# Engine assignments of 714 operations read from a table, beside a new order of operations

## The chip, the cores and the metric

One core of a Trainium2 chip runs the whole program. The metric is the device time of one execution in microseconds (us), as the median of several runs. The core has TensorE (PE, matrix products, with its weight loads shown apart as PEld), VectorE (DVE), ScalarE (ACT), GpSimd (POOL) and SyncE (SP, which issues most transfers). Each engine runs its own instructions strictly in the order in which the program gives them.

## The reference

Three stages follow each other; all is float32 at the boundary.

```
q, k, v: 4 batches x 8 heads x 576 rows x 64          (attention)
  q, k rotated by position (cos, sin tables); scores = q k^T / 8
  attn = exp(scores - rowmax) / (rowsum + 1e-9);  x = attn v      -> 2304 x 512
h = x w_in;  g = max(h,0) + alpha*min(h,0);  y = g w_out           w_in 512x2048, w_out 2048x512
soft mixture of experts over y: logits = y phi (32 slots),
  softmax over tokens -> slot inputs;  8 experts: relu(s w1) w2;  softmax over slots -> output 2304 x 512
```

## The kernel before, in words

The program first lists some five thousand operations (`op(engine, cost, due, function, ...)`), each a small group of instructions on one engine, with what it depends on and which buffers it takes. `Plan.order` then decodes a compressed text, `ORDER`, into a permutation of that list, checks that it respects dependencies and buffers, and the operations are emitted in that order. So the order in each engine's queue, and in SP's queue of transfers, is written out in full; the engine of an operation is fixed in the code. The `cost` and `due` arguments no longer decide anything.

**Weights of the first layer** (`prep_w`): eight pieces of w_in arrive as 64-bit floats and are turned to float32 by three DVE steps (lines 673, 675, 677); ACT finds the bound (685), scales to a float16 high part (688), makes a scaled diagonal `dg` (`split`, 244), PE subtracts (250, 251), and ACT copies the low part (256). Eight more pieces, of w_out, get the same three DVE steps. **Queries and keys** (`prep_qk`): for each of 4 batches and 4 head pairs, POOL multiplies by the two tables (334) and adds (337, or 342 in batch 0). In batches 1 to 3 the sum is split in a high part (ACT: 350 for keys, 352 for queries) and a low part (POOL: 357, 359), and ACT spreads the key's high part into four places (362). **Rows** (`row_events`): PE makes scores (434 in batch 0; 443 to 447 later), DVE finds the negated maximum (452), ACT takes exp with its sum (457), ACT adds 1e-9 (473), DVE takes the reciprocal (474), POOL multiplies (498, and 497 for the tail rows). In batch 0 PE transposes the result (521, 572) and ACT copies it out (531, 576); in batches 1 to 3 DVE transposes blocks (508, 542) and two transfers through memory finish the turn. **Attention times v** (`pv_events`): PE (604), then ACT writes the high part (614), DVE the low part (617). **First layer** (`chunk_events`): 9 blocks of 256 tokens by 16 chunks; PE makes 12 products (766), ACT takes the relu of the negated sum into `rl` (774), DVE forms `g` (779), DVE transposes pairs of chunks (795). After a block, PE makes logits (803) and slot sums (958). The experts come at the end, with their weights loaded once the attention buffers are closed.

The functions that the change touches, and what calls them:

Of the kernel before, what the change touches and what calls it, by code (L numbers as in the profile page):

```python
# [33 lines left out]

ORDER = (
    "c-"
    "mD~2Urx>7M?S+yX?|2bX1gHRZyNvF=9a}V#E>@e8EKHdzz>u8ly;*XDo>rC5a`L_$(MD8XHRS0TQez(t;?`EHove%L2mg&b(V@7u@+~=FUCm{O3RC+`Z@i<x|abJZJsVy~d{s04%K9(G"
    "#p5cvrJp?-$T9|GpAT1M<P-C2u>bTnSxvZPu*P%=hF%DB+-"
    "VM46wm=jF&ILo=DhV{ip!cO{G+{s63(N><uEvE&r1mrieoYPWW|iK^2+XZnj$Uz27Jrnxf^ioBWu?3NsAdF}qf$WisAbkTn!I>5qOecZ|1?~w^uR{2T0tH8TxQu(NI%Y=Dj{k6^Q-"
    "VZE!jve0A;#KVfVEwWLrZ)|~3L0Mkd&rtsVy`qCeSAp$D7X$r9(6wO${w0S>Wd}*kQ1Wp02Amo_P=JPa&f8q6In+h?!L+v!BZZ;sRMi$ulBqgUt?X>2mw7Qsj4ayWk3r&54e}N+vuqh{"  # L40
    "u=y`y9|u%gPb9$Co<>t7~b?Nvu+Ej98oFrtGEY4{F?@AjSS)b=*jsdV-60n0yd-"
    "`I^UR&=xlE?Q}VSRLq*5L!)_CbhP(ab99pC`4=e}CIh!C2SiWv(UJQqp98$Tq1~xzlJR4eT(BM@)e9R5-"
    "?S@9Vyy8ww^Quy)ALf|}#=v@l^5Iheug<KEgRVdH>ikF9B!I@}Aq!6|j8BihxbdNKE<Axd^RmM;T)@?&)S~3ap{t#jpR0WH7-s)5yBvZl!56NFJj-`}?p5~hF<XP5$DNRX-"
    "O<TzP0(d*e^>>JjhX|$N&uzX_St{Tw1;12n8Wd<qdr~k&)2%%2rI7vhrMf3A=*tjp-3{eSljuNVFp{j_LGyxVNQ2=@$ax>WaXNO?RnSF?B0}VvLZ^pvg-"
    "hBRHCIdv%MTfR;*jTH|$!<CU>y)H<SNn;jf&XsMz$-rS6eO`Ztx&OUm{uA=7`_?G*MB#GI&lS{wRiTGvZhe(CI-Xo2UmBe_f=I!8SNzJBfTRkPLAiCGZtx%~APyVmXdJTufR)-"
# [12 lines left out]
    "Q4g}hu13IjPIG&u8fkXOw(5dKuTHG{<^pi{0?pswGGc*B)4lCK0Iq3{;PHLp@E4a<OEO`{SIYUS-{!#j9UAGW1(3Jzc5{1K;q)gq)70#(<doq5DOxAkUQfP;GThV##S6^ZuM9FW+n-"
    "Ta`RuccBhT2y*G03i<;i|IBov;8dba$7yeUl&$Cw|RY5rzXahr^ffKzj0lAEsv4@-}4>*0pAfL-gv%NGZ8!W^iL$$?4LvB%!V9S&Z4??BuxH{}8&h-;l^(sF%4pL-oVHG?-"
    "!4fd^I)jG6wyzIPJwXuoHB!BYHA6f1ET*fM#7A?=44Qvm1KVg7Td9rtnj2)q|+h|x#p9wfV^XUHSpJ48GCIaA!Y1kue*(_GZJ{rod+TUB-"  # L60
    "r<!nQ9F#x}<V|p?8(kk&?ZL^)%KTvD+r<mR1-8(9e8Wp$C~2Ko9C0h?cZXd^6>P2vj0eaz7y}jX!e;!ec{4JHq16OYZ{P+5wHd>=t4!|)!Na3a3_rsin04NE=-tWHp-"
    "`lep$tm6KBR4+;SE@U?KR}NZs%5TuD3A;RhzBx?-5TPIGa^SytxMwiDa<$r5(#TJmWws0pJQ8oo>Bvz^ZtemghKD1qK`o|1<0{4dW!*!r<41U_GAu`%Zv;n-"
    "yrKZMIJhSg7)}d13prV>ByBxxUuH+TF3&lvburu1!Or??8x&mDv-G3%6xx9B6VRy&nMVW@Bv-%NBcyR`T7tANmZ|yyfJ)=0doU=5m8;>w0dz;YZT+__e>bTP3DJ+mWQLNhpr1S-"
    "T`(f9ecJKCV5owHDcDFKckwwR&f(Y|)P^O>B~ePD!|)QKL9ta6H1Y%VODPXg~d>{L8I!mXm%UwcHJgURaPJSMxKk^3j+2<Pe$7@kJBZHo3XdqFFAN_ZqI>2AbT+D^YXK!=jn9djEj=Q}"
    "TM@dw>VNg%h>FRrx^KxDu7Zk8i9A=Pgysj(@n%7oP^txn((w1Z$wbSFgZ8VxBuzBej9&*QefpJz1@(?>ux4iHbbj_ODf%Dd9#i?B0NtZ(5yBz8QoDd;gvf*&hO%wxX(f9zaFHQMmiDKf"
    "tHPQ#1EI@^}Pq+Fe+eMdn>xl$#qsCb-t3>xVDjvrxXQ35E`>LOtZU(V&jr9w%t^eg#k+SnSi_P;KTQ?=$V@-"
    "m(S;odzK5G6pCa1NvXysB(zxkx6=3FzAs=d*x~wBan*`$P@i^PdbNQJbD1p5`foD;u$g|3gUp#8DSg15)gno5D0{z)6~N=7?XVQx>-"
    "h)U=$GWjqLz^0xwcP=)Ax%I(F2dNP!3JmMUq1vgZYsvJf5Ud=O&j#yoYw0I$PFPc4B)BP`|_nhDH{7qDJ`Vg#O=5SomDWejFX-"
    "SJ|61)in@E8#H$!VYnm0*J2hr;Z2F5Oguf`WVp$yW&X}fPfNMUAgcib%donh-IM~IG?)oFruwUN=zOdXhjktAd%42ijfEmWv&Mn%Zl{`NiQ%GwM5Mb2uGquG6|y=@J&O<Dr$P^>L!*(1"
# [27 lines left out]
class Plan:  # L97
# [1499 lines left out]
```

## Time and profile before

| what | value |
|---|---|
| median of 3 runs | 570.95 us (568.36 to 573.3) |
| the profiled execution | 566.88 us, its span 565.1 us |
| busy over the span | PE 531.3 (94%), DVE 449.7 (80%), ACT 348.8 (62%), POOL 321.9 (57%) |
| chain that ended last | PE 75%, ACT 3%, DVE 2%, DMA 1%, issue 1% |
| granted TensorE clock | 0.996 of full speed over the span |
| transfers | 160.76 MB, mean 284 GB/s |

The span runs from the first to the last instruction. Busy time of PE is modelled at its ends. A row that names a line is a group of like instructions; the time after the bar is the group's sum and the mean of one.

### The profile page before, as it was taken

What the parts mean: (1) busy time and instruction counts of PE and PEld (TensorE: products, weight loads), DVE (VectorE), ACT (ScalarE), POOL (GpSimd) and SP (SyncE); (2) the same over time, 40 slices, a digit from 0 to 9 for tenths busy, and PEclk for the clock granted to TensorE, in tenths of its full rate; (3) what the DMA queues carried; (4) which work ended last, traced back from release to release, by engine and by line L of the source; (5) the groups of instructions that cost most, each with busy time, mean ns of one, the idle gap of its engine ahead of it and who ended that gap; (6) DMA issues with size and microseconds to landing.
All of it is one profiled execution on the core that took longest, in us unless ns stands there. A gap on an engine that the chain in (4) does not pass through costs nothing.

```text
span 565.1 us, 14815 instructions
## 1 busy us (share of the span) xinstructions
PE 531.3 (94%) x5770; PEld 394.9 (70%) x5770; DVE 449.7 (80%) x985; ACT 348.8 (62%) x879; POOL 321.9 (57%) x299
## 2 busy tenths in 40 slices
PE   3789998999999999999999999999999999999994
PEld 1455555678888787788787788868778888864463
DVE  5699978878998878889889798888864799843551
ACT  2799977899868767787786787667432222430131
POOL 0989996988989876887886787844300000001000
PEclk9999999999999999999999999999999999999998
DMA  8893945435899988698989789889665999899997
GB/s 300 309 361 118 328 123 181 135 119 167 293 337 333 332 282 314 194 333 287 327 294 339 252 287 319 266 262 327 226 227 179 411 407 406 290 372 391 403 327 226
DMA packets 80806, 160.76 MB, mean 284 GB/s; under 512 B 5344, under 2 KB 44640, under 8 KB 80736
## 3 DMA queue, kind: packets, MB, share of 16 engines
q1 hardware_dynamic: 79408, 158.99, 80.6%
q8 instruction: 46, 0.75, 0.5%
q10 hardware_dynamic: 1328, 0.82, 0.5%
q14 instruction: 24, 0.20, 0.1%
HBM read 115.75 MB, written 36.96 MB: 270 GB/s over the span
## 4 chain that ended last, share of the span: by engine, by line
PE 75%; ACT 3%; DVE 2%; DMA 1%; issue 1%; DVEq 0%; ACTq 0%
PE ph L766 33%; PE pv L604 11%; PE st L447 9%; PE pu L958 4%; PE lg L803 3%; PE ph L1289 2%; PE po L1348 2%; DMA ett<-sc 1%; PE st L443 1%; PE pf L1473 1%; PE st L445 1%; PE pt L521 1%; PE lgt L863 1%; ACT ks L362 1%; ACT e L457 1%
## 5 line engine op out<-in xcount | busy, mean ns | idle before, releaser
L766 PE MATMUL ph<-xt,w 128*128 128x256 f16 x1536 | 184.2, 273 | 0.5 <-DVE xt L617 0.5
L766 PEld LDWEIGHTS <-w 128*128 128x128 f16 x1728 | 161.9, 98 | 30.2 <-issue 7.4
L498 POOL TENSOR_SCALAR e<-e,mm 128x576 f32<-128x576 f32 x144 | 125.5, 881 | 70.3 <-DVE mm L474 66.7
L457 ACT ACTIVATE e<-st,mm 128x576 f32<-128x576 f32 x144 | 106.3, 739 | 37.1 <-DVE mm L452 31.3
L452 DVE TENSOR_REDUCE mm<-st 128x1 f32<-128x576 f32 x144 | 106.2, 742 | 20.1 <-PE st L447 11.7
L774 ACT ACTIVATE rl<-ph 128x256 f32<-128x256 f32 x144 | 53.5, 380 | 69.7 <-PE ph L766 63.9
L334 POOL TENSOR_TENSOR xn<-xn,tabs 128x576 f32<-128x576 f32 x60 | 89.4, 1502 | 6.9 <-DMA xn<-in_k_dram 3.0
L779 DVE SCALAR_TENSOR_TENSOR g<-rl,oma,ph 128x256 f32<-128x256 f32 x144 | 65.7, 465 | 21.3 <-ACT rl L774 20.6
L604 PE MATMUL pv<-ET,vt 128*64 128x256 f32 (+1 forms) x640 | 76.5, 384 | 0.1
L508 DVE STREAM_TRANSPOSE tb<-e 128x512 f32<-128x512 f32 (+1 forms) x108 | 74.8, 704 | 1.7 <-DMA sc<-tb 0.8
L447 PE MATMUL st<-ks,qs 128*128 128x288 f32 x384 | 74.6, 317 | 1.1 <-ACT ks L362 0.9
L604 PEld LDWEIGHTS pv<-ET,vt 128*64 128x64 f32 (+1 forms) x640 | 43.1, 136 | 25.8 <-issue 5.8
L447 PEld LDWEIGHTS st<-ks,qs 128*128 128x128 f32 x384 | 54.5, 189 | 4.6 <-issue 1.6
L795 DVE STREAM_TRANSPOSE gb<-g 128x512 f32<-128x512 f32 x64 | 43.9, 693 | 0.2
L434 PE MATMUL st<-ks 64*128 64x288 f32 (+1 forms) x168 | 30.2, 455 | 11.0 <-DVE ks L307 7.6
L978 POOL MEMSET edt<- 128x256 f32 x1 | 0.3, 313 | 68.4 <-DVE lp L947 68.4
L359 POOL TENSOR_TENSOR qs<-xn,qs 64x576 fp32r<-64x576 f32 x24 | 33.9, 1413 | 7.7 <-ACT qs L352 3.1
L337 POOL TENSOR_TENSOR xn<-xn 128x576 f32<-128x576 f32 x24 | 36.9, 1537 | 0.9
L362 ACT ACTIVATE ks<-xn 64x576 fp32r<-64x576 f32 x48 | 32.6, 680 | 0.7
L434 PEld LDWEIGHTS st<-ks 64*128 64x128 f32 (+1 forms) x168 | 17.2, 191 | 20.8 <-DVE ks L307 8.4
L614 ACT ACTIVATE xt<-pv,vb 128x256 f16<-128x256 f32 x32 | 15.1, 472 | 22.3 <-PE pv L604 21.5
L457 ACT ACTIVATION_READ_ACCUMULATOR e<-st,mm 128x1 f32 x144 | 28.5, 198 | 0.0
(171 smaller groups left out, 782.1 us busy)
## 6 DMA issues: line engine op xcount, KB each, us to landing
sc<-tb SPq DMA_DIRECT2D x48, 576.0 KB, 4.6
ET<-sc SPq DMA_DIRECT2D x24, 1152.0 KB, 7.3
xw<-in_moe_w_dram SPq DMA_DIRECT2D x42, 512.0 KB, 8.4
xn<-in_k_dram SPq DMA_DIRECT2D x15, 576.0 KB, 6.5
xn<-in_q_dram SPq DMA_DIRECT2D x15, 576.0 KB, 4.5
wraw<-in_moe_w_in_dram SPq DMA_DIRECT2D x8, 1024.0 KB, 8.4
wraw<-in_w_out_t_dram SPq DMA_DIRECT2D x8, 1024.0 KB, 6.0
wor<-in_moe_w_out_dram SPq DMA_DIRECT2D x16, 512.0 KB, 10.0
```

Source lines behind the costliest of these rows:

```text
L334: eng.tensor_tensor(e["x"][:, w], e["x"][:, w], tabs[:, w], ALU.mult)
L434: nc.tensor.matmul(st[to, j, at:at + w], x, k[rows, z:z + w], start=True, stop=True)
L447: nc.tensor.matmul(st[:, j, 0:288], r["q"][:, 768 * h + 128 * s:768 * h + 128 * s + 128].bitcast(F32R), r["k"][:, a, h, ks].bitcast(F32R), ...
L452: nc.vector.tensor_reduce(c["mm"][:, h:h + 1], c["st", h][:, :, 0:288], axis=AX.XY, op=ALU.max, negate=True)
L457: nc.scalar.activation(c["e"][:, h].rearrange("p (a n) -> p a n", a=2), c["st", h][:, :, 0:288], AF.Exp, bias=c["mm"][:, h:h + 1], accum_o ...
L498: nc.gpsimd.tensor_scalar(c["e"][:, h], c["e"][:, h], c["mm"][:, 6 + h:7 + h], 1.0, ALU.mult, ALU.mult)
L508: nc.vector.transpose(out=to if tail else to[:, :, 0:8].rearrange("p q (m h) j -> p q m h j", h=2)[:, :, :, h], in_=e.rearrange("p (m q j) ...
L604: nc.tensor.matmul(pv[r], v[k, 4 * h + i if i < 4 else 8 + (h if b else 0)], x, start=(i == 0), stop=(i == 4))
L766: nc.tensor.matmul(ph, wi[j][:, wp, kc, 128 * fo:128 * fo + 128], xt[:, xp, kc, :], start=(n == 0), stop=(n == 3 * KC - 1),)
L774: nc.scalar.activation(c["r"], c["ph"], AF.Relu, scale=-1.0)
L779: nc.vector.scalar_tensor_tensor(blk["g", j][:, fo, :], c["r"], oma[:, f:f + 1], c["ph"], ALU.mult, ALU.add)
L795: nc.vector.transpose(out=blk["gt", j // 2][:, f % 8 - 1:f % 8 + 1, :].rearrange("p c n -> p (c n)"), in_=blk["g", j][:, fo - 1:fo + 1, :] ...
```

## The change

A table of 714 digits, `ENGINES`, is added, and `plan.choose(a, b, ...)` reads the next digit and returns the engine at that place; digit 0 is in every place the engine that the operation had before. `ORDER` is replaced by another text. The helpers `copied` and `times` give the same copy or scaling on any of the engines. The transfers, the matrix products, the maxima, the exps and the transposes on DVE stay on their engines.

Counting the digits in the order in which the program reads them gives these assignments (before, then after):

| operation (line) | before | after |
|---|---|---|
| normalize a head's rows (498), 128 | POOL | POOL 65, ACT 57, DVE 6 |
| the same for tail rows (497 and 498), 16 | POOL | POOL 6, ACT 9, DVE 1 |
| add 1e-9 (473), 80 | ACT | ACT 58, DVE 22 |
| copy out transposes, batch 0 (531, 576), 56 | ACT | ACT 48, DVE 8 |
| high part of attention output (614), 48 | ACT | ACT 22, DVE 26 |
| multiply by tables (334), 60; add (337, 342), 30 | POOL | POOL 54, DVE 6; POOL 26, DVE 4 |
| high part of keys (350) 12, of queries (352) 24 | ACT | ACT 6, POOL 5, DVE 1; ACT 10, POOL 12, DVE 2 |
| low part of keys (357) 12, of queries (359) 24 | POOL | POOL 11, DVE 1; POOL 23, DVE 1 |
| spread keys (362), 48 | ACT | ACT 20, POOL 26, DVE 2 |
| relu of the negated sum (774), 144 | ACT | ACT 112, DVE 32 |
| weights: scale (688) 8, diagonal (244) 8, low part (256) 16 | ACT | ACT 7, DVE 1; ACT 3, POOL 5; ACT 14, DVE 2 |

In batch 0, 17 of 32 normalizations and 3 of 4 of the tail go to ACT, and 6 of the 18 table operations to DVE. Of the 32 relu that go to DVE, 15 are in blocks 0 to 5.

```diff
+ENGINES = (
+    "020000110000000002000200020012001000010202101121200120000012001011000000200020200100120002020011001000010102000002000000"
...
 ORDER = (
...
+    def choose(self, *engines):
+        self.chosen += 1
+        return engines[int(ENGINES[self.chosen - 1])]
...
+    def copied(on, dst, src):
+        if on == ACT:
+            nc.scalar.activation(dst, src, AF.Copy)
+        else:
+            engines[on].tensor_copy(dst, src)
+
+    def times(on, dst, src, scale):
+        if on == ACT:
+            nc.scalar.activation(dst, src, AF.Copy, scale=scale)
+        elif on == DVE:
+            nc.vector.tensor_scalar(dst, src, scale, None, ALU.mult)
+        else:
+            nc.gpsimd.tensor_scalar(dst, src, scale, 1.0, ALU.mult, ALU.mult)
...
-            o = op(on, cost, d, lambda mul=mul: mul(0), [o, *tabs_op], uses=[sx])
+            on = choose(POOL, DVE)
+            o = op(on, cost, d, lambda mul=mul, on=on: mul(0, on), [o, *tabs_op], uses=[sx])
...
-                        o = op(ACT, 640, d + LEADS[0], lambda spread=spread, h=h, up=up: spread(h, up), [o, y], uses=u)
+                        on = choose(ACT, DVE, POOL)
+                        o = op(on, 640, d + LEADS[0], lambda spread=spread, h=h, up=up, on=on: spread(h, up, on), [o, y], uses=u)
...
+            if on == ACT:
+                nc.scalar.activation(to, of, AF.Identity, bias=eps[:, 0:1])
+            else:
+                nc.vector.tensor_scalar(to, of, 1e-9, None, ALU.add)
...
+            on = choose(POOL, DVE, ACT)
...
-                nc.gpsimd.tensor_scalar(c["e"][:, h], c["e"][:, h], c["mm"][:, 6 + h:7 + h], 1.0, ALU.mult, ALU.mult)
+                times(on, c["e"][:, h], c["e"][:, h], c["mm"][:, 6 + h:7 + h])
...
-            nc.scalar.activation(dst(0), c["pv"], AF.Copy, scale=viv[b][:, 1:2])
+            times(on, dst(0), c["pv"], viv[b][:, 1:2])
...
+            if on == ACT:
+                nc.scalar.activation(c["r"], c["ph"], AF.Relu, scale=-1.0)
+            else:
+                nc.vector.tensor_scalar(c["r"], c["ph"], -1.0, 0.0, ALU.mult, ALU.max)
```

## Rows read from the trace of the kernel before

**Rows 1.** Four stretches: length; busy PE, PEld, DVE, ACT, POOL; PE clock, DMA share, GB/s.
```profile
0.00:120.00 120.00, 99.09 (x657) 58.90 (x659) 100.33 (x175) 95.03 (x224) 97.72 (x76) 1.00 0.67 232
120.00:420.00 300.00, 297.83 (x3409) 238.25 (x3410) 259.07 (x587) 214.75 (x558) 221.50 (x219) 1.00 0.83 280
420.00:500.00 80.00, 80.00 (x976) 65.84 (x974) 63.58 (x135) 24.22 (x67) 0.72 (x3) 1.00 0.88 332
...
500.00:565.10 65.10, 54.39 (x735) 31.88 (x733) 26.69 (x89) 14.80 (x33) 1.90 (x2) 0.97 0.94 341
```

**Rows 2.** Chain of waits, 240.9 to 244.5: start us, us, what.
```profile
241.59 0.53 PE st L447 x4
242.12 1.33 PE ph L766 x12
```

**Rows 3.** PE's waits, 0 to 120: total us, times, longest.
```profile
PE st L434 <- DVE ks L307: 7.6, 2, 6.9
PE st L434 <- ACT e L457: 3.4, 3, 2.1
PE pt L521 <- POOL e L498: 3.3, 4, 1.6
PE top L212 <- POOL e L498: 1.8, 1, 1.8
```

**Rows 4.** PE's waits, 120 to 500.
```profile
PE pv L604 <- DMA ett<-sc: 1.3, 1, 1.3
PE ph L766 <- DVE xt L617: 0.5, 2, 0.3
```

**Rows 5.** POOL's groups, 0 to 120: busy us, mean ns | idle before, releasers.
```profile
L498 POOL TENSOR_SCALAR e<-e,mm 128x576 f32<-128x576 f32 x35 | 44.1, 1268 | 19.7 <-DVE mm L474 19.3
L334 POOL TENSOR_TENSOR xn<-xn,tabs 128x576 f32<-128x576 f32 x19 | 31.7, 1683 | 0.3 <-issue 0.3
```

**Rows 6.** POOL's groups, 120 to 500.
```profile
L498 POOL TENSOR_SCALAR e<-e,mm 128x576 f32<-128x576 f32 x109 | 81.5, 757 | 50.6 <-DVE mm L474 47.3 <-ACT rl L774 1.0
L359 POOL TENSOR_TENSOR qs<-xn,qs 64x576 fp32r<-64x576 f32 x22 | 31.1, 1414 | 7.5 <-ACT qs L352 3.1 <-issue 2.8 <-POOL xn L337 0.4
```

**Rows 7.** DVE's groups, 0 to 120.
```profile
L675 DVE SCALAR_TENSOR_TENSOR w<-wraw,w 128x1024 int32<-128x1024 int32 x11 | 16.9, 1541 | 0.2
L302 DVE TENSOR_TENSOR xn<-xn,tabs 128x576 f32<-128x576 f32 (+2 forms) x4 | 2.9, 756 | 5.0 <-DMA xn<-in_k_dram 4.1 <-DMA tabs<-in_rope_dram 0.8
```

**Rows 8.** Timeline of all engines: start us, us, engine, what.
```profile
13.33 1.23 DVE L675 SCALAR_TENSOR_TENSOR w<-wraw,w 128x1024 int32<-128x1024 int32 x1
14.73 2.43 POOL L498 TENSOR_SCALAR e<-e,mm 128x576 f32<-128x576 f32 x2 [13.03 <-DVE mm L474]
```

**Rows 9.** ACT's groups over the whole span.
```profile
L350 ACT ACTIVATE xn<-xn 128x576 fp32r<-128x576 f32 x12 | 8.1, 677 | 0.3 <-POOL xn L337 0.3
L473 ACT ACTIVATE mm<-mm,eps 128x2 f32<-128x2 f32 (+1 forms) x80 | 23.1, 293 | 1.3
L531 ACT ACTIVATE ET<-pt 128x512 f32<-128x512 f32 x32 | 18.7, 594 | 3.5 <-PE pt L521 3.3
L614 ACT ACTIVATE xt<-pv,vb 128x256 f16<-128x256 f32 x32 | 15.1, 472 | 22.3 <-PE pv L604 21.5
L774 ACT ACTIVATE rl<-ph 128x256 f32<-128x256 f32 x144 | 53.5, 380 | 69.7 <-PE ph L766 63.9 <-DVE wo L1128 2.2 <-DVE g L779 1.9
```

**Rows 10.** DVE's groups, 120 to 500.
```profile
L967 DVE COPY acc<-pu 128x256 f32<-128x256 f32 x4 | 1.4, 402 | 0.0
L1124 DVE TENSOR_SCALAR wo<-wor 128x512 int32<-128x512 int32 x16 | 6.6, 418 | 0.1
L474 DVE RECIPROCAL mm<-mm 128x2 f32<-128x2 f32 (+1 forms) x61 | 8.4, 145 | 3.6 <-ACT mm L473 3.6
```

**Rows 11.** DVE's waits over the whole span.
```profile
DVE g L779 <- ACT rl L774: 20.6, 38, 2.1
DVE xt L617 <- ACT xt L614: 14.8, 11, 3.7
```

More of the change, by code (lines that the diff above doesn't have):

```diff
@@ L195, in attn_moe_softmoe @@
         wf=1, rl=2, g=2, wt=1, lp=1, lt=1, edt=2, dn=1, dg=2, x=29, h1=2, mov=2, tmp=1))
-    op = plan.op
+    op, choose = plan.op, plan.choose
     PE, ACT, DVE, POOL, DMA = "PE", "ACT", "DVE", "POOL", "DMA"
+    engines = {ACT: nc.scalar, DVE: nc.vector, POOL: nc.gpsimd}
+    def copied(on, dst, src):
[10 more added lines that the diff above has]
+            nc.gpsimd.tensor_scalar(dst, src, scale, 1.0, ALU.mult, ALU.mult)
     FIRST = -10000.0
@@ L240, in split, with diag @@
         half = int(dg[0] is not None)
-        def diag():
+        on = choose(ACT, DVE, POOL) if dg[0] is None else None
+        def diag(on=on):
             e["d"] = wst.tile([128, 128], F32, tag="dg", name="dg", bufs=2)
-            nc.scalar.activation(e["d"], idf, AF.Copy, scale=scale())
+            times(on, e["d"], idf, scale())
         def mults():
@@ L251, in mults @@
             nc.tensor.matmul(ps, neg["t"], hi, start=False, stop=True)
-        o = op(ACT, 250, due, diag, [dep, neg_op], takes=[s_d], uses=[s_d]) if dg[0] is None else dg[2]
+        o = op(on, 250, due, diag, [dep, neg_op], takes=[s_d], uses=[s_d]) if dg[0] is None else dg[2]
         dg[:] = [s_d, e, o]
         o = op(PE, n * 2.1, due - ATT, mults, [o, dep, after], takes=[s_p], uses=[s_d, s_p] + uses)
-        return op(ACT, 595, due, lambda: nc.scalar.activation(dst(1), e["p", half], AF.Copy), [o, after], uses=[s_p] + uses)
+        on = choose(ACT, DVE)
+        return op(on, 595, due, lambda on=on: copied(on, dst(1), e["p", half]), [o, after], uses=[s_p] + uses)
     vt, viv, viv_op = {}, {}, {}
@@ L323, in prep_qk @@
             return
-        eng, on, cost = nc.gpsimd, POOL, 1570
+        cost = 1570
         for i, (src, z) in enumerate(((kx, "k"), (qx, "q"))):
@@ L377, in prep_qk @@
             o = order_ops["load"] = op(DMA, 1700, d, load, [order_ops["load"]], takes=[sx], uses=[sx])
-            o = op(on, cost, d, lambda mul=mul: mul(0), [o, *tabs_op], uses=[sx])
-            o = op(on, cost, d, lambda mul=mul: mul(1), [o], uses=[sx, s_tabs])
+            on = choose(POOL, DVE)
+            o = op(on, cost, d, lambda mul=mul, on=on: mul(0, on), [o, *tabs_op], uses=[sx])
+            on = choose(POOL, DVE)
+            o = op(on, cost, d, lambda mul=mul, on=on: mul(1, on), [o], uses=[sx, s_tabs])
+            on = choose(POOL, DVE)
             if not b:
                 prev = order_ops.get("k")
-                o = op(on, cost, d, whole, [o, prev], takes=[s_st["k"]] if z == "k" else [], uses=[sx, s_st["k"]])
+                o = op(on, cost, d, lambda whole=whole, on=on: whole(on), [o, prev], takes=[s_st["k"]] if z == "k" else [], uses=[sx, s_st["k"]])
                 order_ops["k"] = o
@@ L521, in turn, with turned @@
                     nc.tensor.transpose(c["pt", h][:, i], c["e"][:, h, 64 * h + 128 * i:64 * h + 128 * i + 128], idf)
-            def turned(h=h):
+            on = choose(ACT, DVE)
+            def turned(h=h, on=on):
                 if tail:
@@ L537, in row_events @@
             pair.setdefault("turn", o2)
-            evs.append(op(*((DVE, 690) if h and b else (ACT, 600)), n + h + LEADS[2], turned, [o2] + evs[:1], uses=[s_pm, s_ET]))
+            evs.append(op(on, 600, n + h + LEADS[2], turned, [o2] + evs[:1], uses=[s_pm, s_ET]))
         if moved:
@@ L622, in pv_events @@
         x.setdefault("op", o)
-        o = op(ACT, 130 if tail else 470, FIRST + n, evac_hi, [o, viv_op[b], x.get("first")], uses=u_)
+        o = op(on, 130 if tail else 470, FIRST + n, evac_hi, [o, viv_op[b], x.get("first")], uses=u_)
         x.setdefault("first", o)
@@ L685, in bnd, with hi @@
             nc.scalar.activation(dst(0), xv(), AF.Abs, accum_out=mw[:, 0:1])
-        def hi():
-            nc.scalar.activation(dst(0), xv(), AF.Copy, scale=sw[:, j:j + 1])
+        on = None if which else choose(ACT, DVE)
+        def hi(on=on):
+            times(on, dst(0), xv(), sw[:, j:j + 1])
         even = w_ops.get((which, j - 1)) if j % 2 else None
@@ L711, in prep_w @@
         scale_ops[j] = o
-        o = scaled = op(ACT, 1040, due + WS, hi, [o], uses=[s_wx, s_w])
+        o = scaled = op(on, 1040, due + WS, hi, [o], uses=[s_wx, s_w])
         dg = [None]
@@ L817, in chunk_events @@
             blk["g_taken"] = o
-        o = op(ACT, 385, d, below, [o], takes=[s_r], uses=[s_pm, s_r])
+        o = op(on, 385, d, below, [o], takes=[s_r], uses=[s_pm, s_r])
         o = op(DVE, 480, d, act, [o, oma_op, blk["g_op"][4 * j] if fo else None], uses=[s_pm, s_r, s_g])
```

170 lines of the change are left out of this document (92 added, 78 removed).

## The prediction

> **What bounds the kernel now.** I read the four stretches first, because the share of busy time over the whole span mixes different limits. Between 120 and 420 us TensorE is busy 297.8 of 300, between 420 and 500 all 80, at a granted clock of 1.00, which is the 2.4 GHz level [rows 1]. Whatever other engines win there cannot show unless TensorE's few gaps close. Its idle time sits at both ends: 120 - 99.1 = 20.9 us in the first 120, 65.1 - 54.4 = 10.7 in the last 65.1, and 2.2 between; 33.8 in all.
>
> Next I asked whether that busy middle hides slack, since matmul ends are modelled. In the chain of waits a chunk of 12 products takes 1.33 us and four score products 0.53, and the next piece begins at the end of the last: 241.59 + 0.53 = 242.12 [rows 2]. It is dense work.
>
> Then TensorE's waits. In the first 120 us it loses 7.6 us to the first keys, which come from the first loads, 3.4 to exps that hold the score buffers, and 3.3 + 1.8 where the releaser is POOL's normalization [rows 3]. From 120 to 500 the named waits are 1.3 us for one fetch through memory and 0.5 for the output's low part [rows 4]. The last 65 us is a chain of short steps whose engines the table does not touch.
>
> Last I read what fills the first stretch: DVE 100.3, ACT 95.0 and POOL 97.7 of 120 us [rows 1]. Nobody is idle, and POOL is slow there: a normalization costs 1268 ns, and 757 after 120 us [rows 5, 6]; a table product 1683 [rows 5]. DVE's second conversion step took 1.23 us at 13.33, when POOL was still waiting for its first normalization (it begins at 14.73 after 13.03 idle), and averages 1541 ns in the stretch [rows 7, 8]. The two engines slow each other.
>
> **The change, part by part.** The digits move 229 of the 714 operations; no transfer, product or exp changes its engine or size.
>
> *First stretch (weights and batch 0).* POOL loses 20 normalizations, tail ones counted, 20 x 1.268 = 25.4 us, and 6 table operations, 6 x 1.683 = 10.1 [rows 5]. It gains 5 diagonals, at most 5 x 0.757 = 3.8 by the larger normalization [rows 6]. Net -32: 97.7 becomes 66. ACT gains the 20 at 0.677, the price of a copy of the same size, 13.5 us; it loses 7 additions at 0.293, 6 output parts at 0.472, and 16 copies, diagonals and scalings at about 0.594, together 14.4 [rows 9]. Net nothing: 95. DVE gains 6 x 0.756 = 4.5 for the table operations [rows 7], 6 output parts at 0.402, 7 additions at the reciprocal's 0.145, and 11 copies and scalings between that 0.402 and ACT's 0.594 for twice the columns (I take 0.5) [rows 9, 10], together 4.5 + 2.4 + 1.0 + 5.5 = 13.4. Against that POOL is a third less busy. If the three conversion steps each lose in 15 pieces what the second one shows, 1.54 - 1.23 = 0.31, they lose 14 us, and a third of it, 4.6, comes back. DVE: 100.3 + 13.4 - 4.6 = 109.
>
> So the load per engine goes from 100, 95, 98 to 109, 95, 66. The links of a row's chain get shorter where POOL ran them: 1.27 to 0.68 us for a normalization that moves to ACT. What bounds the gain: DVE cannot start before the first load, idle 5.0 us there [rows 7], so the stretch is not under 114 us, a gain of at most 6; by TensorE's waits, 20.9 less the 7.6 and the longest wait for an exp, 2.1 [rows 3], at most 11. I take 5, nearer to DVE's bound because that engine keeps an order of its own and will not be packed fully. The low end is zero, the high end 11.
>
> *From 120 to 500.* DVE gains 32 relu at 0.402 (a read of 128x256 from PSUM), 12.9 us; 20 output parts at most 8.0; 15 additions 2.2; 12 normalizations and copies at 0.418 x 576/512 = 0.47, 5.6; 6 table or low-part operations at 0.756, 4.5 [rows 7, 10]. That is 33 on 322.7: 356 of 380, or 94%. ACT gains 46 normalizations, 31.2, and loses 32 x 0.380, 20 x 0.472, 15 x 0.293 and 48 key and query copies at 0.677, 58.5 in all: 239 becomes 212 [rows 1, 9]. POOL loses 53 normalizations, 40.1, and 6 others at 1.414, 8.5, and gains 43 copies whose price no row shows: between 0.757, an operation of one input and as many columns, and 1.414, one of two inputs [rows 6]. I take 0.757, being nearest in kind: 222 becomes 206, at the other end 234, of 380. These costs I put at nothing, because TensorE covers them; the cover lasts as long as DVE stays under it. A gain of up to 2.2 remains, TensorE's idle time. An output part on DVE saves the hop that made DVE wait 14.8 us for ACT, a relu the hop of 20.6 [rows 11], and the fetch's 1.3 can go by order alone [rows 4]. I take 2.
>
> *Where a wait moves.* POOL's normalizations waited 47.3 us for the reciprocal after 120 [rows 6]; POOL had nothing urgent behind them. On ACT the exps of later rows and the relu that TensorE's next buffers need are queued behind the normalization, so the same wait would hold them. Nothing in the diff's readable part says where in ACT's queue they stand. Keys and queries that POOL spreads stand behind POOL's table products instead.
>
> *The order.* The new text permutes all queues, SP's and POOL's among them, and is not readable. Its worth is bounded above by TensorE's idle time, 33.8 less the 7.6 of the first load and the short chain at the end; below, nothing excludes a loss. For the last 65 us I take zero.
>
> Sum: 5 + 2 + 0 = 7 us. The profiled execution took 566.9, its span 565.1 and 1.8 around it, so 559.9. The median of the runs shown is 4.1 above the profiled time, so 564.0.
>
> **A rule against it.** Rows 5 to 8 show POOL and DVE slowing each other, and the table puts 10 table operations on DVE. The Trainium skill, page "SBUF — State Buffer", section "Who interferes with whom", says that a VectorE instruction with two inputs in SBUF contends with a GpSimd one that reads SBUF, and that one of them waits for the whole of the other. By it each of the six early table operations would cost DVE its 0.756 a second time, 4.5 us: 109 becomes 113.5, with the idle start 118.5, the stretch gains 1.5 in place of 5, and the median comes out at 567.5, still within 1% of before. The trace agrees on the contention (1268 against 757 ns) but shows an average of 0.3 us lost on DVE's side, not a whole instruction.
>
> **Rivals.**
>
> *No change that can be told.* DVE takes the place of POOL as what is late in the first stretch: with its contention unrelieved and the table operations at 0.756 + 0.31, DVE reaches 100.3 + 13.4 + 1.9 = 116, and 5 us of idle start makes 121. For: DVE is the busiest already. Against: POOL's load falls by a third. The gain is 0 to 2: 569 to 571.
>
> *More than I sum.* The table and order together close the 11 us of the start, the 2.2 and some 3 of the end: 571 - 16 = 555. For: three engines at 66 to 109 of 120 leave room for it. Against: DVE's 114. Weight loads fill 238 of the 300 middle microseconds [rows 1], but pieces follow each other without a gap [rows 2]. The Trainium skill, page "Perfetto Trace Analysis", section "Identifying the Most-Contended Engine", holds the weight loads' share for the better measure of TensorE's headroom; by it a fifth of the middle could go, 60 us, which gives about 510, and rows 2 leave that no more than 1 in 100.
>
> *Slower: DVE becomes the bound between 120 and 420.* DVE stands at 259.1 of 300 there [rows 1]; 15 relu instead of 32 make its addition 33 - 6.8 = 26, so 285 of 300, 95%. It decides where a stretch of a chunk or two holds more DVE work than TensorE's 1.86 us per chunk: then TensorE's three product buffers fill and it waits. If a third of the 26 us falls on such places, 9 us come out on TensorE: 571 - 5 + 9 = 575; with no gain at the start 580. For: DVE works through maxima, transposes and `g` in one queue, and every moved relu adds 0.40 where 0.38 ran beside it. Against: DVE also waits 20.6 + 14.8 us for ACT in that work [rows 11], and part of this goes.
>
> **How the numbers follow.** Chances: forecast 0.45, no change 0.25, more 0.12, slower 0.18. A difference within 1%, 5.7 us, is about what a measurement of this kernel cannot tell from none: 565.2 to 576.7. The forecast's own range is 559 (the start's bound of 6 and a little of the end) to 569; six in ten of it lie under 565.2. Faster: 0.45 x 0.65 + 0.12 = 0.41, and a little of the slower case's gain at the start, 0.42. Slower beyond 576.7: most of that case, 0.16. The same: 0.42. The range for 8 in 10 reaches from 554, where most of the larger gain lies, to 576, where half of the slower case is left out.
>
> **What would show it.** Right: in the first 120 us TensorE's idle time falls from 20.9 to about 16, POOL's load to 66, and DVE's second conversion below 1541 ns; the middle stays at 1 us of idle or less; ACT's normalization takes near 0.68, POOL's copies 0.76 to 1.4. Wrong: TensorE's waits between 120 and 420 name DVE for `g`, maxima or output parts with more than 5 us in all (the slower case); or the first stretch shows DVE over 113 and the same idle time (no change); or the copies on POOL take over 1.4 us and TensorE waits for keys.

## The result and the profile after

The changed kernel takes 573.3 us (median of 20 runs, 569.73 to 577.93), the one before 568.2 in the same session (20 runs, 565.86 to 573.3): a ratio of 1.0091 [1.0068, 1.0114], 5.1 us slower. I had forecast 7 us less. The time lies inside the range of 554 to 576 and under the 1% that the prediction called hard to tell, but these runs do tell it, and the sign is the other one; that the range holds it is luck, since its upper end stood there for a mechanism (DVE as the bound) that the runs do not bear out. The forecast of 564.0 also started from a median of three runs, 570.95, where twenty give 568.2. The profiled execution of after took 577.93 us, at the long end of its runs, with a span of 575.3 and a mean granted clock of 0.987; I take sizes from medians and places from the trace. (A slip in the text ahead of the prediction: the program lists 2803 operations, not some five thousand.)

The four stretches of after, columns as in [rows 1]:

```profile
0.00:120.00 120.00, 101.40 (x668) 59.21 (x669) 107.13 (x209) 96.17 (x215) 60.20 (x55) 1.00 0.66 229
120.00:420.00 300.00, 295.26 (x3338) 236.17 (x3348) 277.95 (x642) 202.23 (x511) 199.88 (x193) 0.99 0.84 279
420.00:500.00 80.00, 79.07 (x997) 63.13 (x984) 66.69 (x148) 18.84 (x51) 0.84 (x3) 1.00 0.84 317
500.00:575.30 75.30, 63.23 (x786) 39.96 (x784) 32.67 (x105) 15.77 (x34) 1.90 (x2) 0.93 0.89 319
```

The loads moved as the table says: POOL 97.7 to 60.2 in the first stretch, DVE 259 to 278 in the second. TensorE's idle time falls from 20.9 to 18.6 at the start and rises from 2.2 to 4.7 between 120 and 420, where the prediction wanted 1 or less. Its waits in the first 120 us, beside [rows 3]:

```profile
PE st L478 <- DVE ks L343: 8.5, 2, 7.9
PE st L478 <- ACT e L501: 2.3, 2, 1.7
PE rest L285 <- ACT w L219: 2.3, 3, 0.9
PE top L245 <- ACT w L743: 1.7, 2, 1.2
PE pt L576 <- POOL e L229: 0.4, 1, 0.4
```

The waits for POOL's normalization, 5.1 us before, are down to 0.4. In their place stand 4.0 us in which TensorE waits for ACT's pieces of the weights, `w`; before, those waits came to 0.7 and 0.2 us. ACT now also has normalizations in that queue, but in none of the five waits does one stand just ahead of the piece. In two of them, the 1.7 us for the bound of a piece (L743), ACT itself stands idle for DVE's last conversion step. In the other three, 2.3 us for low parts (L219), a bound of v, a bound of another piece and an exp stand ahead; why the order has these late was not tested.

```profile
15.77 1.06 ACT L743 ACTIVATE w<-w 128x1024 f16<-128x1024 f32 x1 [2.23 <-DVE w L735]
40.22 1.06 ACT L743 ACTIVATE w<-w 128x1024 f16<-128x1024 f32 x1 [1.18 <-DVE w L735]
```

From 120 to 420, beside [rows 4]:

```profile
PE ph L826 <- DVE g L844: 2.3, 1, 2.3
PE st L491 <- issue: 1.2, 1, 1.2
PE st L491 <- POOL qs L395: 0.4, 1, 0.4
```

In the last stretch, before and then after:

```profile
PE pf L1473 <- DVE mov L1378: 0.9, 1, 0.9
PE pf L1473 <- DVE ob L1478: 0.5, 1, 0.5
```

```profile
PE pf L1538 <- DVE mov L1443: 2.8, 3, 1.3
PE pf L1538 <- DVE ob L1543: 1.0, 2, 0.8
```

The 2.3 us for `g` between 120 and 420 are one event. DVE is named, but it is not where it begins. ACT's queue at that place, in time order (start us, us, what, idle before and releaser):

```profile
226.30 0.36 ACT L940 ACTIVATE lt<-lgt 32x256 f32<-32x256 f32 x1
229.55 0.74 ACT L314 ACTIVATE junk<-vt 128x640 f16<-128x640 f32 x1 [2.89 <-DMA vt<-in_v_dram]
230.19 0.19 ACT L314 ACTIVATION_READ_ACCUMULATOR junk<-vt 128x1 f32 x1
230.28 0.76 ACT L225 ACTIVATE e<-e,mm 128x576 f32<-128x576 f32 x1
230.95 0.64 ACT L837 ACTIVATE rl<-ph 128x256 f32<-128x256 f32 x2
```

and DVE's and TensorE's there:

```profile
231.08 0.71 DVE L563 STREAM_TRANSPOSE tb<-e 128x512 f32<-128x512 f32 x1 [2.82 <-ACT e L225]
231.71 0.44 DVE L844 SCALAR_TENSOR_TENSOR g<-rl,oma,ph 128x256 f32<-128x256 f32 x1
...
228.77 1.15 PE L826 MATMUL ph<-xt,w 128*128 128x256 f16 x9
232.20 4.45 PE L826 MATMUL ph<-xt,w 128*128 128x256 f16 x24 [2.29 <-DVE g L844]
```

Read from the top: the operation at the head of ACT's queue is the bound of a piece of v (L314: it sums magnitudes, from which a scale is made), which could stand 22 places later without harm (r3 below); its load is late, so ACT stands for 2.89 us. Behind it are a normalization, for which DVE's transposes wait 2.82, and two relu, without which DVE can make no `g`; so TensorE's product buffers fill. Then the clock pays too: two stretches of 4 us across the gap, columns as in [rows 1].

```profile
228.00:232.00 4.00, 1.92 (x18) 1.57 (x16) 1.18 (x3) 2.45 (x7) 3.77 (x5) 1.00 1.07 346
232.00:236.00 4.00, 3.80 (x22) 2.82 (x22) 3.97 (x11) 3.81 (x10) 1.52 (x2) 0.63 0.81 306
```

The granted clock falls to 0.63, a mix of the 2.4 and 1.2 GHz levels, and 24 products take 4.45 us where the trace of before has 2.79: 1.7 us more behind a gap of 2.3.

```profile
228.68 2.79 PE L766 MATMUL ph<-xt,w 128*128 128x256 f16 x24
```

In the last stretch TensorE waits 2.8 + 1.0 us for `mov` and output copies; before it was 0.9 + 0.5. (`mov` holds the experts' results, which go into the last products.) The table doesn't touch these operations: only their order is new.

### The profile page after: what moved, and what is told of

Read it like the earlier page. It is cut to its first block, busy times and chain, and to the rows that moved or that the text cites. A ratio compares the mean times of both kernels' runs of the same rounds, so it can differ in the third digit from the quotient of the medians.

```text
span 575.3 us, 14788 instructions
## 1 busy us (share of the span) xinstructions
PE 539.0 (94%) x5770; PEld 398.5 (69%) x5770; DVE 484.4 (84%) x1101; ACT 333.0 (58%) x810; POOL 262.8 (46%) x252
## 4 chain that ended last, share of the span: by engine, by line
PE 59%; DVE 12%; POOL 11%; DMA 7%; ACT 6%; issue 3%; SPq 2%; DVEq 0%; POOLq 0%; ACTq 0%
PE ph L826 22%; PE pv L660 9%; PE st L491 5%; PE pu L1023 3%; POOL xn L370 3%; PE po L1413 2%; PE lg L868 2%; PE pt L576 2%; PE st L478 2%; POOL e L229 2%; DVE mm L496 2%; PE ph L1354 2%; DMA vt<-in_v_dram 2%; PE rest L285 2%; POOL xn L373 1%
## 5 line engine op out<-in xcount | busy, mean ns | idle before, releaser
L501 ACT ACTIVATE e<-st,mm 128x576 f32<-128x576 f32 x144 | 106.2, 739 | 48.4 <-DVE mm L496 44.9
L229 POOL TENSOR_SCALAR e<-e,mm 128x576 f32<-128x576 f32 (+1 forms) x77 | 60.4, 789 | 78.3 <-DVE mm L527 69.9
L370 POOL TENSOR_TENSOR xn<-xn,tabs 128x576 f32<-128x576 f32 x54 | 80.0, 1492 | 24.4 <-DMA ks<-xn 14.1
L837 ACT ACTIVATE rl<-ph 128x256 f32<-128x256 f32 x112 | 41.3, 378 | 73.3 <-PE ph L826 65.7
L225 ACT ACTIVATE e<-e,mm 128x576 f32<-128x576 f32 (+1 forms) x75 | 53.3, 721 | 4.3 <-DVE mm L527 3.9
L395 POOL TENSOR_TENSOR qs<-xn,qs 64x576 fp32r<-64x576 f32 x23 | 32.6, 1417 | 19.6 <-ACT qs L219 10.7
L373 POOL TENSOR_TENSOR xn<-xn 128x576 f32<-128x576 f32 x22 | 31.4, 1431 | 4.0 <-DVE xn L370 3.1
L1043 POOL MEMSET edt<- 128x256 f32 x1 | 0.3, 311 | 69.8 <-DVE lp L1012 69.8
L576 PE MATMUL pt<-idf,e 128*128 128x128 f32 x144 | 22.1, 287 | 2.3 <-DVE mws L248 0.9
```

The costliest lines, as they stand in the source:

```text
L225: nc.scalar.activation(dst, src, AF.Copy, scale=scale)
L229: nc.gpsimd.tensor_scalar(dst, src, scale, 1.0, ALU.mult, ALU.mult)
L370: engines[on].tensor_tensor(e["x"][:, w], e["x"][:, w], tabs[:, w], ALU.mult)
L501: nc.scalar.activation(c["e"][:, h].rearrange("p (a n) -> p a n", a=2), c["st", h][:, :, 0:288], AF.Exp, bias=c["mm"][:, h:h + 1], accum_o ...
```

## The experiments

Each version was timed beside the kernel before, whose median was 567.3 to 568.0 us; ratios are to it, and differences of a few us between versions are taken from the ratios. "Order" is the decoded list of 2803 operations, "digits" the table.

**The two halves of the change.** First the new order with every operation on its old engine.

```diff
-ENGINES = ( the 714 digits )
+ENGINES = "0" * 714
```

> The changed kernel's order with every table digit at 0, so that each operation is on the engine it had before. Theory A (the new order carries the loss: the changed kernel's stalls near 230 us and in the last 20 us are put there by the order): this stays slower than before by 4 to 9 us, with its normalizations back on POOL. Theory B (the table carries the loss, through VectorE's load, 484 us in place of 450): this is within 2 us of the kernel before. If order and table only fit together, it is the worst of the four, by over 10 us.

617.02 us, 1.0892 [1.0841, 1.0942]. POOL's normalizations, all back in its queue, wait for the reciprocal with the rest of POOL's work behind them:

```profile
L222 POOL TENSOR_SCALAR e<-e,mm 128x576 f32<-128x576 f32 (+1 forms) x160 | 119.5, 756 | 124.1 <-DVE mm L520 109.3 <-DVE inv_w L198 5.1 <-PE ph L819 4.8
```

Then the new digits in the old order.

```diff
-ORDER = ( the text of after )
+ORDER = ( the text of before )
```

> The order of before with the new table. Theory A: within 2 us of before or up to 4 faster, TensorE's idle time from 120 to 420 us stays under 3 us although VectorE is as loaded as in the changed kernel. Theory B: slower than before by 4 us or more, TensorE waits for VectorE between 120 and 420. If the two only fit together: slower by over 5 us, with waits at the moved normalizations.

605.56 us, 1.0672 [1.0622, 1.0723]. Now ACT's queue is the wrong one; TensorE's waits over the span:

```profile
PE pt L575 <- ACT e L224: 9.3, 7, 2.5
...
PE st L477 <- ACT e L500: 5.5, 4, 2.3
PE st L490 <- ACT e L500: 3.8, 7, 1.2
PE ph L825 <- DVE g L843: 3.7, 7, 1.0
```

Both came out as the case that the two only fit together. Neither half is the cause by itself: by the medians one alone costs 49 us, the other 38, together they cost 5. Each of these two written-out orders fits its own assignment and not the other. So a gain of the table and a loss of the order, which I had set against each other, cannot be told apart that way.

**The v bound later.** In the new order the bound of ACT is dealt out 22 places later.

```diff
 load of v, quarter 3            place 1175
-ACT bound of v, quarter 3       place 1189
 ACT bound of v, quarter 2       place 1211
+ACT bound of v, quarter 3       right behind it
```

> The changed kernel with one operation moved in ScalarE's queue: the bound of one piece of v in batch 2, which waits 2.9 us for its load near 229 us with a normalization and two relu queued behind it, now stands after the next bound, some twenty operations later. Theory A1 (this wait holds the queue and makes TensorE wait 2.3 us for g and lose clock after it): the gap of TensorE between 228 and 232 us goes, the granted clock there stays at 1.00, 2 to 5 us faster than the changed kernel. Theory B (VectorE's load is what is late): no change within 1 us, the same gap moves a few us on.

571.77 us, 1.0074 [1.0042, 1.0107]. The gap is not in its trace, and the clock there stays at 1.00, but the time falls by 1.5 us only, under the 2 to 5 of theory A1 and within the noise of one comparison. Why so little of 2.3 + 1.7 comes back shows in the other kernels that keep the bound in its place. ACT's wait there in the runs r4, r6 and e10 below, one line of each:

```profile
228.16 0.74 ACT L269 ACTIVATE junk<-vt 128x640 f16<-128x640 f32 x1 [1.58 <-DMA vt<-in_v_dram]
230.81 2.78 PE L781 MATMUL ph<-xt,w 128*128 128x256 f16 x24 [0.98 <-DVE g L799]
```

```profile
227.77 0.74 ACT L262 ACTIVATE junk<-vt 128x640 f16<-128x640 f32 x1 [1.31 <-DMA vt<-in_v_dram]
230.43 2.78 PE L774 MATMUL ph<-xt,w 128*128 128x256 f16 x24 [0.71 <-DVE g L792]
```

```profile
231.22 0.74 ACT L262 ACTIVATE junk<-vt 128x640 f16<-128x640 f32 x1 [1.41 <-DMA vt<-in_v_dram]
233.87 2.78 PE L774 MATMUL ph<-xt,w 128*128 128x256 f16 x24 [0.81 <-DVE g L792]
```

The same 24 products take 2.78 us there: among these the clock fell only behind the longest gap. Of the versions near the whole change six hold the bound in its new place (after, r4, r6, e10, e11, e12); TensorE loses 2.29, 0.98, 0.71, 0.81, 2.16 and 1.96, 1.5 in the mean. (In r1, r7 and r8, which have it too but run differently, it loses 0.47, 1.34 and nothing.) No such wait is near there in the traces of before, r3, r5, e14.

**The old tail, and both repairs.** 231 operations at the end, in the relative order that they had before.

```diff
-order[2568:], operations common to both ends: new sequence
+order[2568:], operations common to both ends: old sequence
```

> The changed kernel with the order of before for 231 operations of the last 60 us (experts, combination, output), nothing else moved. Theory A2 (the order of the output's products leaves TensorE idle and its clock low in the last 20 us): the stretch from the last product of the first layer to the end falls from 69.7 us to about 66, 2 to 4 us faster than the changed kernel. Theory B: no change within 1 us.

570.44 us, 1.0048 [1.0023, 1.0073]: 2.4 us come back by the ratios (0.0043 of 568), as theory A2 said, with an uncertainty of some 2. Its trace has the waits of before again:

```profile
PE pf L1493 <- DVE mov L1398: 0.9, 1, 0.9
```

Then both edits at once:

> The changed kernel with both repairs of the order: the bound of v in batch 2 placed later, and the order of before for the last 231 operations. Theory A (the loss lies in places of the order): the two gains add, 1.5 + 2.9, so about 569 where the changed kernel took 573.3, within 1 us of before. Theory C (one thing stands behind both, the clock that falls after any gap): no more than the better of the two, 570.4.

569.28 us, 1.0022 [0.9992, 1.0052]. The time is that of theory A, the two gains added, and what is left can no longer be told from before; theory C's 570.4 lies inside the interval too, so that they add is likely and not shown.

**Is DVE the bound?** The 32 relu that moved to DVE go back to ACT, nothing else.

```diff
-ENGINES: 32 digits of the relu = 1 (DVE)
+ENGINES: the same digits = 0 (ACT)
```

> The changed kernel and its order, but the 32 relu that went to VectorE are back on ScalarE; VectorE's load falls by about 13 us, to 471. Theory B (VectorE's load bounds): 2 us or more faster than the changed kernel. Theory A (each queue's order fits one table): slower than the changed kernel by 1 to 10 us, because each relu stands behind ScalarE's exps and normalizations at a place that was chosen for another queue.

572.46 us, 1.0098 [1.0067, 1.0128], as the whole change, with DVE 12 us less busy: neither theory's difference appears. These 12 of the 35 us by which DVE's load grew are not what costs, unless ACT lost as much by taking the relu back at places that were chosen for DVE; the other 23 us were not tested.

**Two more moves taken back**, 73 digits of the normalizations, and 50 of keys and queries, all to 0.

> The changed kernel and its order, but the 73 groups of normalizations that left POOL are back on it (66 from ScalarE, 7 from VectorE). Theory A: slower by 10 us or more, most of the 44 us that all digits at 0 cost, because POOL's queue holds table products and key copies between a reciprocal and its normalization, and TensorE waits for transposes of the result. Theory B: within 3 us of the changed kernel, as ScalarE had room for them either way.

605.49 us, 1.0651 [1.0603, 1.0698], theory A. DVE's and TensorE's longest new waits:

```profile
DVE tb L511 <- POOL e L177: 15.2, 15, 3.1
...
PE st L439 <- POOL qs L343: 5.5, 5, 2.9
```

> The changed kernel and its order, but the 50 copies and low parts of keys and queries are back on the engines of before (48 leave POOL or VectorE for ScalarE). Theory A (TensorE's score weights wait for keys that POOL spreads): the waits of the score products for POOL fall, yet ScalarE's queue now holds exps behind copies that wait for POOL's sums; between 2 us faster and 10 us slower than the changed kernel, the sign being open. Theory B: within 2 us.

591.07 us, 1.0397 [1.0351, 1.0444], more than either theory allowed; POOL's low parts wait for ACT's high parts:

```profile
POOL qs L343 <- ACT qs L167: 31.9, 10, 7.9
```

In excess of the whole change these cost 32 and 18 us, the relu none: 50, near the 44 by which r1 exceeds it. So most of the new order's dependence on the table seems to lie in those two moves.

**Where the loss sits.** Both orders have dealt out the same operations, but for 3 to 8, after 723, 1120, 1344, 2032 and 2597 places (in the trace of before TensorE passes them at 145, 214, 255, 379 and 520 us). So a kernel can be new up to such a place and old behind it, digits included.

```diff
-order[0:723] and its digits: before
+order[0:723] and its digits: after
```

> The new order and the new engines for the first 723 operations alone (up to about 146 us, 74 of the 229 moved operations), where both orders have dealt out the same work but for 3 operations; the old order and the old engines for the other 2080. Theory L (the start gains about 2 us, the loss of 5 lies behind it): 566, some 2 us under the kernel before, ratio 0.995 to 0.999, first gate product near 120.5 us. Rival S (the start gains nothing, the first product only comes earlier and the work behind it later): 568, ratio 1.000. Rival J (the joint between two orders costs by itself, since a new start leaves engines ahead or behind of where the old rest expects them): 570 or more.

566.41 us, 0.9965 [0.9935, 0.9995]: the start alone gains 2.0 us, as theory L said, and this version beats both kernels, if narrowly: the interval reaches to 0.3 us.

```diff
-order[723:2597] and its digits: before
+order[723:2597] and its digits: after
```

> The old order and engines for the first 723 operations, the new ones from there to about the last gate product (154 moved operations), the old order again for the last 206. Theory L: the queue stall near 229 us and the waits for keys stay, 1.5 + 2.7 on the kernel before: 572, ratio 1.007, the time of the whole change less its tail (570.4) plus the start's 2. Rival S: 570.4 as with the old tail, ratio 1.004 to 1.005. Rival J (joints): 574 or more.

572.37 us, 1.0070 [1.0038, 1.0102], again theory L. The next two extend the new part from the start to 1344 and to 2032:

> The new order and engines for the first 1344 operations (to about 255 us, with the late v bound near 229 us in it), the old for the rest. Theory L, the loss sits at the queue stall: -2 + 1.5 to 3, so 567.5 to 569, ratio 0.999 to 1.002; the waits for keys of later batches are not in it. Rival K (the keys and queries lose evenly over the four batches): two of the four batches lose 1.3, with the stall the same 568 to 569, and the version with 2032 operations then loses more. If both parts of the loss lie before 255 us: 570.4, as the whole change with the old tail.

570.62 us, 1.0044 [1.0011, 1.0077], the last of the three cases.

> The new order and engines for the first 2032 operations (to about 382 us, 190 moved operations), the old for the rest. Rival K, keys and queries lose evenly over the batches: some 1 us more than the version with 1344, 569 to 570. If the stall near 229 us is all that the middle loses: the same as with 1344, within 1 us. If the loss sits between 382 us and the last gate product: under 569 here against 570.4 for the whole change with the old tail.

569.69 us, 1.0031 [1.0006, 1.0055], the same as with 1344 within 1 us. In this series the ratio stands at 0.9965 after 723 places, 1.0044 after 1344, 1.0031 after 2032, 1.0048 after about 2568 (r4) and 1.0091 at the end. The loss is made twice: 4.5 us between places 723 and 1344, and 2.4 in the tail, each with an uncertainty of some 2 us. From 1344 to the tail nothing is lost that these intervals could show.

**Is the first of these the v bound alone?** The new part ends ahead of the bound; then it goes to 1344 with the bound later.

```diff
-order[0:1344] and its digits: after
+order[0:1120] and its digits: after
```

> The new order and engines for the first 1120 operations (112 moved), up to some 15 us ahead of the v bound on which ACT waits near 230 us; the old for the rest. Theory W (the middle's loss is that one wait): as with the new start alone, 566 to 567, ratio 0.996 to 0.999. Rival K (small waits for keys, queries and output parts behind the start add up): 568.5 to 570, ratio 1.002 to 1.004.

570.72 us, 1.0043 [1.0012, 1.0073].

```diff
-order[0:1344]: after
+order[0:1344]: after, with the bound of v behind place 1211
```

> The version with the first 1344 operations new (570.6, ratio 1.0044), with that one v bound dealt out 22 operations later, right behind the other bound of its kind; nothing else. Theory W: the whole 4 us that TensorE loses there come back, 566.5, ratio 0.997 to 0.999, and the trace shows no wait for g. Rival K: about 1.5 us come back as in the whole change, 569, ratio 1.002.

569.71 us, 1.0035 [1.0006, 1.0064]: 0.5 us come back of theory W's 4. By the times alone theory W, the one wait, is out, and all of the loss is there by place 1120. The trace of e13 says otherwise on the place. There TensorE passes place 1120 at 214.6 us, and its two longest waits up to place 1344, for a fetch through memory, come right behind it:

```profile
216.35 2.38 PE L608 MATMUL pv<-ET,vt 128*64 128x256 f32 x20 [1.77 <-DMA ET<-sc]
221.36 2.38 PE L608 MATMUL pv<-ET,vt 128*64 128x256 f32 x20 [0.68 <-DMA ET<-sc]
```

That is the old order, which has no such wait there in the trace of before: these 2.5 us come with the joint, and e13 does not show that the new order loses them ahead of the bound. What it does lose there differs from trace to trace: in after between 147 and 227 us the waits are 0.2 each, for DVE, an exp and POOL, beside 1.2 within a group of four products with no releaser, and e9, old there, has such 1.2 as well, between products of `pv`. No single cause holds in all.

**Joining the parts that lost nothing.**

```diff
-order[723:1344], order[2032:] and their digits: after
+order[723:1344], order[2032:] and their digits: before
```

> The new order and engines for the operations up to 723 and from 1344 to 2032 (130 moved), the old between and after: the parts that lost nothing by the runs so far. If the parts add: -2.0 - 0.7, 564.7, ratio 0.994 to 0.997, faster than before and than the new start alone. If the gain of 0.7 was noise: 565.4 to 566, ratio 0.997. If the joints cost: 567 or more.

567.27 us, 0.9999 [0.9977, 1.0021]: the parts do not add to 2.7. Whether the start's 2 us are gone is not shown, since this interval and that of e9 overlap. And the bound's stretch alone in the old kernel:

```diff
-order[1120:1344] and its digits: before
+order[1120:1344] and its digits: after
```

> The kernel before with the new order and engines from operation 1120 to 1344 alone (20 moved digits), the stretch in which ACT waits for the v load. Theory W: TensorE's wait for g of about 2.3 us appears in it, and 2 to 4 us more in all: 569.5 to 571.5, ratio 1.004 to 1.007. Rival K: 1 to 1.5 us, 568.5 to 569. If the stall needs the new queue ahead of it (the load is dealt out at another moment here): no wait for g, 567.4, ratio 1.000.

576.92 us, 1.0150 [1.0112, 1.0187], 8.5 us and more than either theory allowed, without a wait for `g`. But its trace shows the same kind of wait, made by the joint. Another bound of v (quarter 1) here stands 12 places behind its load, where it stands 102 places behind in the order of before and 119 in that of after. It heads ACT's queue for 3.58 us, with an exp behind it on which TensorE waits 3.48, and the granted clock falls behind that gap, from 1.00 to 0.66 (last line, columns as in [rows 1]):

```profile
221.48 0.74 ACT L262 ACTIVATE junk<-vt 128x640 f16<-128x640 f32 x1 [3.58 <-DMA vt<-in_v_dram]
223.08 0.80 PE L439 MATMUL st<-ks,qs 128*128 128x288 f32 x4 [3.48 <-ACT e L449]
```

```profile
223.00:227.00 4.00, 3.67 (x16) 2.41 (x18) 2.97 (x8) 3.69 (x11) 3.85 (x5) 0.66 0.33 127
```

So a joint between two orders can cost by itself, 2.5 us in e13 and 3.5 in e16, more with the clock, and times of parts alone cannot place a loss better than that. All of e16's loss this is not: its trace is 3.3 us behind that of before already at place 723, where both kernels have the same order, and that part stays open.

**The places in the traces.** TensorE runs its products in the order of the list, so counting the products of a trace along the list tells when the last one ahead of a place ends, and two places give the time of the stretch between. Means in us (lowest to highest; number of traces), without r1, r2, r7 and r8:

| places | old order there | new order there |
|---|---|---|
| 0 to 723 | 146.2 (144.6 to 147.9; 3) | 144.4 (143.2 to 145.8; 11) |
| 723 to 1120 | 70.4 (69.8 to 70.8; 4) | 71.4 (70.3 to 74.2; 10) |
| 1120 to 1344 | 40.3 (40.3 to 40.3; 3) | 42.7 (41.6 to 44.9; 6); with the bound later 41.2 (40.7 to 41.7; 3) |
| 1344 to 2568 | 255.1 (254.0 to 255.9; 6) | 254.5 (253.5 to 255.7; 6) |
| 2568 to the last product | 48.7 (48.6 to 49.1; 8) | 52.2 (50.7 to 54.6; 3); with the old tail 50.0 (49.8 to 50.2; 3) |

(e13 and e16, which change orders at 1120, are not in the third row, e12 and e15, which change at 2032, not in the fourth.) The start gains 1.7 us. The middle loses 1.1 ahead of place 1120 and 2.4 behind it, of which 1.5 go with the bound. The tail loses 2.0 and 2.5 in r3 and r6, and 5.8 in after. The sum, 4.5, is near the 5.1 of the medians. Each trace is one execution, and the three with the same old start differ by 3.3 us; the third and the last row, where the old order varies by half a microsecond at most, are the firm ones.

## Why the prediction was wrong

**The step that failed** is the one on the order: "below, nothing excludes a loss. For the last 65 us I take zero", together with "These costs I put at nothing, because TensorE covers them" and the 2 us of gain in the middle. Measured: the tail loses 2.4 (r4) and the middle some 4 in place of gaining 2 (4.0 by e10, 4.5 by e9 and e11). With the start's -2.0 that is 4.4 to 4.9 of the 5.1. Some 1 to 1.5 us of the middle are the v bound: 1.5 by TensorE's waits in six traces and by the table above, 1.0 by the mean of the three pairs with and without it (1.0091 and 1.0074, 1.0048 and 1.0022, 1.0044 and 1.0035), none of which is clear of noise by itself. Of the rest the traces put 1.1 ahead of place 1120 and 0.9 behind it; its cause is open. I had costed the middle by load, with TensorE as cover: DVE at 94%. The part of the load that was tested, the relu, is not it (r6). What the traces show instead is an operation at the head of a queue whose input is late (after, and again e16), and the loads in the trace of before cannot show that of a queue that is yet to be written. Nor does the list alone: in the order of before the same bound stands 16 places behind its load, in that of after 14, and ACT waits there only in the new one.

**The first stretch** had the right mechanism and the wrong size: 5 predicted, 2.0 measured. The loads came out near the working: POOL 60 (66 predicted), ACT 96 (95), DVE 107 (109), so DVE's bound of 114 was not what limited it. For DVE that is luck in part: its three conversion steps took 52 us in place of 61, so 9 came back where the sum had 4.6, and what was added came to some 16 in place of 13.4. I removed POOL's waits, 4.7 us of the 5.1 went, and did not price the waits that would take their place: 4.0 us for weight pieces instead of 0.9.

**Where a wait moves** asked the right question, and I gave it no number. It says that on ACT the exps and relu are queued behind the normalization. In the trace the normalization's own wait for the reciprocal is small there, 2.9 us for 66 of them over the span against 47.3 for 109 on POOL before [rows 6]; that the new order puts it late enough would fit, but was not tested. The wait that holds ACT is a load's.

```profile
L225 ACT ACTIVATE e<-e,mm 128x576 f32<-128x576 f32 x66 | 50.2, 772 | 3.3 <-DVE mm L527 2.9
L221 POOL CAST ks<-xn 64x576 fp32r<-64x576 f32 x23 | 16.1, 699 | 1.1
L839 DVE TENSOR_SCALAR rl<-ph 128x256 f32<-128x256 f32 x29 | 11.9, 412 | 5.2 <-PE ph L826 4.6 <-ACT e L225 0.3
L733 DVE SCALAR_TENSOR_TENSOR w<-wraw,w 128x1024 int32<-128x1024 int32 x11 | 13.8, 1258 | 0.1
```

**The prices** were near, and decided nothing: ACT's normalization 0.77 (0.68 taken), POOL's copies 0.70 (0.757, the lower bound), relu on DVE 0.41 (0.40), and the second conversion step fell from 1541 to 1258 ns, nearly the 1.23 of one beside an idle POOL [rows 8], with POOL 38% less busy. The first step fell too, from 1040 to 702 ns, but the third did not, 1450 and 1467.

**The rule against it.** A table product on DVE takes 892 ns in the first 120 us where such operations took 756 before [rows 7], at 5 to 9 us, while POOL stood idle [rows 8]. The two additions of that size take 1120:

```profile
L370 DVE TENSOR_TENSOR xn<-xn,tabs 128x576 f32<-128x576 f32 x5 | 4.5, 892 | 0.0
L378 DVE TENSOR_TENSOR ks<-xn 128x576 f32<-128x576 f32 x2 | 2.2, 1120 | 0.0
```

That is 0.14 us of loss in the mean for a product and 0.36 for an addition, not the whole 0.756 a second time. The Trainium skill, page "SBUF — State Buffer", section "Who interferes with whom", has the two engines exclude each other there; that they disturb each other agrees with these rows, a whole instruction of waiting for each of the moved operations doesn't.

**The rivals.** "Slower: DVE becomes the bound" gave 575 to 580, the right sign and nearly the size, by a mechanism that the runs do not bear out: DVE's waits for the relu fell from 20.6 [rows 11] to 6.0, giving the relu back changes nothing (r6), and TensorE's waits that name DVE between 120 and 420 come to 2.5 us, where the rival asked for more than 5 and where 2.3 of them begin on ACT.

```profile
DVE g L844 <- ACT rl L837: 6.0, 12, 1.0
```

"No change" named DVE at 116 in the start; it reached 107. "More" had nothing to it, nor had its 510 us by the share of the weight loads.

## What to carry to other kernels

An order written out for every queue can be fitted closely to one assignment of engines: here taking back 73 normalizations under the new order cost 32 us, taking back 32 relu nothing. Test the pair together, and judge it by what heads each queue when an input is late, not by loads or the price of an operation alone. Where a stall is named for one engine, go back along the queues to the operation at the head; here an early bound on a late load held relu that TensorE needed 2 us later. A new order can be cut at places where both have done the same work, so the parts are timed by themselves, but the joint can cost too; the traces of the parts, read between the same places, say where.

## What the hardware showed that I had not expected

A gap of 2.29 us in a dense stretch was followed by a granted clock of 0.63 and 1.7 us of slower products, nearly the gap again; behind gaps of 0.7 to 2.2 us in five other traces the same products took their 2.78. The gap's length alone does not settle it: in e14 one of 2.20 us, up to 198.5 us, was followed by 4 us at 0.58, in e11 one of 2.16 by 4 us at 1.00. The end of the profiled execution of after shows a low clock too (columns as in [rows 1]); in the trace of before, 550 to 560 us stand at 1.00.

```profile
555.00:560.00 5.00, 3.95 (x26) 3.68 (x27) 2.52 (x5) 1.96 (x4) 0.00 (x0) 0.73 0.89 288
560.00:565.00 5.00, 5.00 (x107) 4.62 (x110) 0.00 (x0) 0.92 (x2) 0.00 (x0) 0.58 0.89 260
```

r3, which has the same new tail, stands at 1.00 from 545 us to its last product, with the same waits for `mov` and output copies, 2.8 + 1.0 us, and r6 at 1.00 from 545 to 563. From place 2568 on they take 50.7 and 51.2 us and after 54.6. So the low clock cost that tail some 3.5 us, an estimate from these three; with the middle's 1.7 it is about the 4.6 by which this execution exceeds the median. What made the clock fall in the one tail and not in the others stays open.
